# A late stage of attention without weight conversion, and a first token list made in two halves

## The chip, the cores and the metric

The kernel runs as one program on one core of a Trainium2 chip. The metric is the device time of one execution in microseconds (us). The engines are named as the profile names them: PE (TensorE), PEld (its weight loads), DVE (VectorE), ACT (ScalarE), POOL (GpSimd) and SP (SyncE, which here only issues DMAs). They run beside each other, each through its own list of instructions in a fixed order.

## The reference

```
x   = windowed attention(q, k, v)            # 4 x 8 heads, 576 rows, window 128, slope bias
logits = x @ w_gate                          # 2304 tokens x 8 experts
# greedy: (token, expert) pairs by falling logit; a token goes once, an expert takes at most 288
for e in experts: out[tokens of e] = relu(x[tokens] @ w1[e]) @ w2[e]
y = (silu(out @ w_gate2) * (out @ w_val)) @ w_out        # 512 -> 1536 -> 512
```

Each expert takes exactly 288 tokens, so the greedy choice can be made expert by expert: the expert that fills up first is found, its 288 tokens are listed, they are taken out, and so on, eight times.

## The kernel before, in words

**Two plans.** All work is described as tasks: engine, modelled duration, due time, what is read and written. `Plan.run` takes the tasks, always starts the one that can start first by its model, prefers early due times among those that can start about together, and so writes the order of every engine's list. There are two runs of it. The first covers attention (`plan.run(FIT[0], need)`): it ends when every attention task (`need`) is placed, and it fills gaps with the conversion of GLU weights (`glu_weights`, chunks 0 to `EARLY_GLU - 1`). The second covers everything else. The model holds no clock changes of PE and no lock between DVE and POOL other than its own "port".

**GLU weights.** 36 chunks of 512 KB go through three staging buffers (`stg`). On DVE each takes a shift (L329), a join (L332) and a sum (L344, or L348 for the last twelve chunks); for the first 24 DVE then forms the low half (L357). ACT does two conversions per chunk (L298). Chunks from `EARLY_GLU` on are loaded after the first gathers; chunks in `HOLD` get a tiny POOL memset into their buffer first (`hold`), which stands behind the gathers in POOL's list, so that SP can't start their load earlier.

**Attention.** 80 steps (4 batches x 5 row blocks x 4 head pairs). A step does scores on PE (L550), the maximum on DVE (L558), the exponential on ACT (L564), transposes on PE (L570), the split of the result in a high and a low float16 half, and products with the values on PE (L610). The split is done by ACT and DVE (L581, L585). In the steps of `VIA` (n mod 5 is 2 or 4) it goes by ACT (L590), POOL or DVE (L301) and POOL (L598). Every second step is followed by a normalization: ACT copies the sums (L654), DVE takes the reciprocal (L657), scales (L662) and sums the logits (L666). The normalized rows are stored to `x_dram` by SP.

**The first list, `route(0)`.** A chain on DVE, with a product on PE in each link: a search in six digits (compare L766, in two halves for the first list; count on PE L773; L841, PE L847, next digit), then positions (L882 to L928). Then `onehot` (L931) compares `k_slot`, a float16 table [128, 128, 18], with the positions, and `listed` (L936) makes the list with 18 small products, one for each of 18 tiles; `listed2` (L941 to L945) writes the indices. `k_slot` is filled once, by POOL (L301, called at L723). `CH` is cleared by POOL (L719). Gaps of the chain are filled with weight conversions. For the planner the chain can't start until all constants are there, `k_slot` among them; the instructions themselves wait for it only at `onehot`.

**The first expert.** `tokens(0)` issues three gathers on POOL (L1103: two of 128 rows of 2 KB, one of 128 quarter rows). Between the list and the gathers' landing stand `WARM` tasks: 12 products of no use (L1117), which keep PE busy. PE then turns the rows around (L1128, nine transposes in three pieces), ACT and DVE copy them (`X`), and the products of the expert follow (L1179: two layers in float32 for the first expert; L1174: GLU; L1309: output). For the seven later experts the lists, gathers and turns are made in the middle of the previous expert's products; the planner puts a turn where its model says that the gather has landed: `LATE` = 1.6 us after the transfer.

Of the kernel before, what the change touches and what calls it, by code (L numbers as in the profile page):

```python
# [9 lines left out]
F32 = mybir.dt.float32  # L10
F16 = mybir.dt.float16
# [38 lines left out]
FIT = (0.2, 0.1)  # L50

VIA = (5, (2, 4))
WARM = 6
EARLY_GLU = 11
HOLD = range(11, 14)

STEPS, FINE = (6, 6, 5, 5, 5, 5), (2, *10 * (3,))

# [66 lines left out]
class Plan:  # L125
# [15 lines left out]
    def add(self, engine, us, due, fn, r=(), w=(), late=0.0, soft=False, port=False):  # L141
        t = {"on": engine if isinstance(engine, dict) else {engine: us}, "due": due, "fn": fn, "late": late, "soft": soft, "port": port,
             "no": self.count, "deps": [], "next": [], "slots": [], "done": None}
        self.count += 1
        deps = {}
        for key in (*r, *w):
            if key in self.writer:
                deps[self.writer[key]["no"]] = self.writer[key]
        for key in w:
            for d in self.readers.get(key, ()):  # L150
                deps[d["no"]] = d
        for key in r:
# [12 lines left out]
        return t  # L165
# [24 lines left out]
                    s = max(s, max(u["done"] + u["late"] + HANDS.get(engine, 0.2) for u in users))  # L190
        return s

    def run(self, fit, need=None, near=0.0):

        todo = [t for t in self.todo if t["done"] is None]
        left = len(todo) if need is None else sum(t["done"] is None for t in need)
        ids = None if need is None else {t["no"] for t in need}
        ready = [t for t in todo if not t["wait"]]
        while left:
            by = {}  # L200
            busy = None if ids is None else {e for t in todo if t["done"] is None and t["no"] in ids for e in t["on"]}
            for t in ready:
                for e, us in t["on"].items():
                    if busy is not None and e not in busy:
                        continue
                    s = self.start(t, e)
                    if s is not None:
                        by.setdefault(e, []).append((t["due"], t["no"], s, us, t))
            best = None
            for e, c in by.items():  # L210
                s0 = min(x[2] for x in c)
                c = [x for x in c if not x[4]["soft"] or x[2] <= s0 + fit]
                first = min(c)
                fits = [x for x in c if x[2] + x[3] <= first[2] + fit or (e == "DVE" and x[2] + 0.1 < first[2] and x[0] < first[0] + near)]
                if fits:
                    s0 = min(x[2] for x in fits)
                    first = min(x for x in fits if x[2] <= s0 + fit)
                if best is None or first[2] < best[0][2]:
                    best = first, e
            (_, _, s, us, t), e = best  # L220
            t["ran"], t["done"] = e, s + us
            self.free[e] = s + us
            if self.ported(t, e):
                self.free["port"] = s + us
            for name in t["slots"]:
                if not self.slots[name]["taken"]:
                    self.slots[name]["taken"] = True
                    self.order[name[0]].append(name)
            ready.remove(t)
            for u in t["next"]:  # L230
                u["wait"] -= 1
                if not u["wait"]:
                    ready.append(u)
            left -= ids is None or t["no"] in ids
            t["fn"](e)
        self.todo = [t for t in todo if t["done"] is None]
        return max(self.free.values())
# [6 lines left out]
def dve(n, lanes=1):  # L244
    return 0.07 + n / 960 / lanes


def pool(n, ins=1):
    return 0.08 + n * ins / 940
# [11 lines left out]
def body(ctx, tc, a, out):  # L261
# [17 lines left out]
    k_tri = const.tile([128, 128], F16, name="k_tri")  # L279
    k_sum = const.tile([128, 3 * E], F16, name="k_sum")  # L280
    logits = const.tile([128, NT, E], F32, name="logits")
    x_dram = dram.tile([N, DM], F32, name="x_dram")

    def load(due, dst, src, nbytes, r=(), w=()):
# [11 lines left out]
    def copy_scaled(engine, dst, src, scale):  # L296
        if engine == "ACT":
            nc.scalar.activation(dst, src, AF.Copy, scale=scale)  # L298
        else:
            eng = nc.vector if engine == "DVE" else nc.gpsimd  # L300
            eng.tensor_scalar(dst, src, scale, 1.0, op0=OP.mult, op1=OP.mult)  # L301
# [75 lines left out]
    with ExitStack() as es:  # L377
# [13 lines left out]
        def due(n, off=0.0):  # L391
            return ATT_US * n + off
# [29 lines left out]
        for b in range(1, B):  # L422
# [7 lines left out]
        add("Pool", 0.2, due(40), lambda e: nc.gpsimd.tensor_copy(k_tri, cst[:, at["tri"]]), [("cst",)],  # L430
            [("cst", "tri")])

        add("Pool", 0.1, due(40), lambda e: nc.gpsimd.tensor_copy(k_sum, cst[:, at["sum"]]), [("cst",)],
            [("cst", "sum")])

# [101 lines left out]
        def step(n, b, kt, hp):  # L537
# [84 lines left out]
            for p in pars:  # L622
# [2 lines left out]
            cols = 128 * len(slots)  # L625
            add("PE", 0.109 * len(slots), due(n, 2.4), turn,
                r=[("ident",), ("PBz", n % NPB)] + [("PB", n, p) for p in pars], w=[("t", n)])
            if n % VIA[0] in VIA[1]:
                vi = vias[0]
                vias[0] += 1  # L630
                add("ACT", act(cols, True), due(n, 3.0), whole, r=[("t", n)], w=[("tf", vi)])
                add({"Pool": pool(cols), "DVE": dve(cols, 2)}, None, due(n, 3.2), high2, r=[("tf", vi)], w=[("th", n)], port=True)
                add("Pool", pool(cols, 2), due(n, 3.4), low2, r=[("tf", vi), ("th", n)], w=[("tl", n)])
            else:
                add("ACT", act(cols, True), due(n, 3.0), high, r=[("t", n)], w=[("th", n)])
                add("DVE", dve(cols), due(n, 3.6), low, r=[("t", n), ("th", n)], w=[("tl", n)])
# [56 lines left out]
        need = list(plan.todo)  # L693
        for c in range(EARLY_GLU):
            glu_weights(c, 2000 + c)
        plan.run(FIT[0], need)

# [12 lines left out]
    def rest_of(k):  # L710
# [3 lines left out]
    csum = const.tile([128, 1], F32, name="csum")  # L714
    bst = const.tile([128, NT], F32, name="bst")
    code = const.tile([128, NT], F32, name="code")
    CH = const.tile([128, NT // 3, 32], F16, name="CH")
    big = ctx.enter_context(tc.tile_pool(name="big", bufs=1))
    add("Pool", 0.7, U0 - 60, lambda e: nc.gpsimd.memset(CH, 0.0), w=[("CH",)])  # L719
    k_slot = big.tile([128, 128, NT], F16, name="k_slot")  # L720

    onehots = big.tile([128, 128, NT], F16, name="oc")
    add("Pool", pool(128 * NT), U0 - 40, lambda e: copy_scaled(  # L723
        e, k_slot, cst[:, at["slot"], None].to_broadcast([128, 128, NT]), 1.0), [("cst",)], [("cst", "slot")])
    rw = ctx.enter_context(tc.tile_pool(name="rw", bufs=2))
    wk = ctx.enter_context(tc.tile_pool(name="mwk", bufs=2))
# [6 lines left out]
    def route(k, due0, due1):  # L733
# [193 lines left out]
            for j in range(3):  # L927
                V.scalar_tensor_tensor(rh[:, :, j], v["pos"], 128.0 * j + 0.5, k_tok, op0=OP.is_gt, op1=OP.mult)  # L928

        def onehot():  # L930
            V.tensor_tensor(onehots, k_slot, v["po"][:, None, :].to_broadcast([128, 128, NT]), op=OP.is_equal)  # L931

        def listed():
            v["pi"] = rp.tile([128, 64], F32, name="rp")
            for t in range(NT):
                nc.tensor.matmul(v["pi"][:, :3], onehots[:, :, t], v["rh"][:, t, :], start=(t == 0),  # L936
                                 stop=(t == NT - 1))

# [78 lines left out]
        do("DVE", 0.7, place2)  # L1017
        do("DVE", 0.6, place3)
        do("DVE", 0.27, place4)
        do("DVE", dve(NT * 128, 2), onehot)  # L1020
        do("PE", 1.2, listed, w=[("listed",)] if k == 0 else [])
        do("DVE", 0.3, listed2, w=[("idx", k)])
        if k < E - 1:
            do("DVE", 0.3, close1)
# [68 lines left out]
    def tokens(k, u):  # L1093
# [14 lines left out]
        for c in range(3):  # L1108
            add("Pool", 1.03, u - ta, lambda e, c=c: fetch(e, c),
                r=[("idx", k)] + [("x_dram", b, kt) for b in range(B) for kt in range(5)], w=[("xg", k, c)], port=None)  # L1110
            add("DMA", 0.55, u - ta, lambda e: None, w=[("xg", k, c)], late=LATE)
        for i in range(WARM if k == 0 else 0):

            def warm(e):
                p = bank()
                for x in range(2):
                    nc.tensor.matmul(p, k_ones, GV[:, 0, 0, x], start=True, stop=True)  # L1117

            add("PE", 0.6, U0 - 30, warm, r=[("listed",)], w=[("mm", ("warm", i))])


        def turn(e, c, kd):
# [10 lines left out]
        for n, piece in enumerate(pieces):  # L1133
            add("PE", 0.11 * len(piece), u - ta + 4 + tn * n, lambda e, piece=piece: [turn(e, *x) for x in piece],
                r=[("xg", k, c) for c, _ in piece] + [("ident",)], w=[("mm", (k, "x", kd), c) for c, kd in piece], soft=k > 0)

        def ends(kd):

# [297 lines left out]
```

## Time and profile before

| | us |
|---|---|
| median of 3 runs (840.08 to 843.21) | 841.53 |
| the profiled execution, its own time | 841.45 |
| its span, first to last instruction | 839.7 |

PE is busy for 94% of the span, DVE for 73%, ACT for 41%, POOL for 17%. The chain of work that ended last spends 39% of the span in the products of L1174 alone. Attention ends near 139 us, the first list and its gathers take until 173 us, and from there to the end products follow one another. Start times are counted from the first instruction; a busy time of an engine over a stretch can be set against the stretch; the number in brackets behind a row of the timeline is the idle time of that engine before it and what ended it. [...]

### The profile page before, as it was taken

To read this page: it belongs to the slowest core of one execution; us is meant where nothing else is said; L and a number is where in the kernel's file an instruction comes from. 1 tells how busy PE (TensorE), PEld (TensorE's weight loads), DVE (VectorE), ACT (ScalarE), POOL (GpSimd) and SP (SyncE) were. 2 spreads that over 40 slices of the span, in tenths; PEclk is the share of its full clock that TensorE was granted. 3 is DMA by queue.
4 is the path that set the end of the run, shared out by engine and by line. 5 is a ranking of instruction groups with operands and counts; after the bars stand their busy time and mean duration, and the time that the engine had idled before them with its cause. 6 is when DMAs were issued, how large, how long until landed. Compare 5 with 4: busy or idle time off the path is not lost.

```text
span 839.7 us, 16655 instructions
## 1 busy us (share of the span) xinstructions
PE 791.2 (94%) x6373; PEld 583.5 (69%) x6373; DVE 614.5 (73%) x1795; ACT 345.2 (41%) x782; POOL 139.4 (17%) x200
## 2 busy tenths in 40 slices
PE   7999995489999999999999999999999999999997
PEld 6888884257774778577767865777677677757763
DVE  3788899979998988788878886889788864312320
ACT  5788884236445724412341243124312453312220
POOL 5677753100001000100110011001100120010001
PEclk9999998589999999999999999999999999999999
DMA  8889612468664002400330043004201561000001
GB/s 271 306 305 329 223 59 82 139 203 282 189 220 153 27 1 101 141 14 1 130 125 1 2 155 113 1 2 160 95 1 35 185 216 49 2 27 1 1 2 38
DMA packets 32064, 92.08 MB, mean 110 GB/s; under 512 B 3952, under 2 KB 10480, under 8 KB 31216
## 3 DMA queue, kind: packets, MB, share of 16 engines
q1 hardware_dynamic: 29008, 81.57, 29.1%
q0 software_dynamic: 2976, 9.44, 3.4%
q8 instruction: 50, 0.82, 0.4%
q14 instruction: 30, 0.25, 0.1%
HBM read 81.56 MB, written 9.44 MB: 108 GB/s over the span
## 4 chain that ended last, share of the span: by engine, by line
PE 55%; issue 10%; DVE 7%; DMA 4%; ACT 1%; POOL 1%; POOLq 0%; SPq 0%; DVEq 0%; ACTq 0%
PE mm L1174 39%; PE mm L1313 9%; PE mm L1179 4%; DMA xg<-x_dram,idx 2%; DMA stw<-in_w_dram 2%; DVE cn L808 1%; DVE cmp L804 1%; PE mm L1309 1%; PE mm L1128 1%; DVE P L1086 1%; PE rp L936 1%; DVE WE L1062 1%; ACT WE L1058 0%; PE rp L812 0%; POOL out_dram L1322 0%
## 5 line engine op out<-in xcount | busy, mean ns | idle before, releaser
L1174 PE MATMUL mm<-O,GV 128*128 128x288 f16 x2304 | 288.2, 286 | 0.5 <-DVE O L1088 0.5
L1174 PEld LDWEIGHTS <-GV 128*128 128x128 f16 x2304 | 221.9, 98 | 56.3 <-issue 0.9
L1174 PEld LDWEIGHTS <-WE 128*128 128x128 f16 x1344 | 130.0, 98 | 34.7 <-issue 1.4
L1313 PE MATMUL mm<-WO,P 128*128 128x512 f16 x504 | 112.9, 379 | 0.0
L1260 ACT ACTIVATE P<-z 128x288 f16<-128x288 f32 x84 | 37.1, 442 | 128.6 <-DVE z L1252 128.4
L1103 POOL DMA_INDIRECT xg<-x_dram,idx x24 | 25.3, 1053 | 386.0 <-PE mm L1174 172.4
L1062 DVE SCALAR_TENSOR_TENSOR WE<-stw,WE 128x512 f16<-128x512 f32 x112 | 74.5, 687 | 17.0 <-ACT WE L1058 17.0
L1313 PEld LDWEIGHTS <-P 128*128 128x128 f16 x504 | 48.9, 98 | 53.8
L1174 PE MATMUL mm<-P,WE 128*128 128x288 f16 x672 | 84.6, 286 | 0.0
L1174 PE MATMUL mm<-X,WE 128*128 128x288 f16 x672 | 83.9, 286 | 0.3 <-ACT X L1157 0.3
L1058 ACT ACTIVATE WE<-stw 128x1024 f16<-128x1024 f32 x56 | 58.5, 1055 | 30.6 <-DMA stw<-in_w_dram 30.5
L1252 DVE SCALAR_TENSOR_TENSOR z<-mm,t 128x288 f32<-128x288 f32 x84 | 38.0, 453 | 41.8 <-PE mm L1174 38.1
L808 DVE TENSOR_REDUCE cn<-cmp 128x56 f16<-128x1008 f16 (+2 forms) x55 | 63.6, 1157 | 0.5
L550 PE MATMUL s<-kt,qb 128*128 128x192 f32 (+2 forms) x288 | 57.4, 334 | 5.2 <-DMA kt<-in_kT_dram 4.2
L804 DVE TENSOR_TENSOR cmp<-wm,thr 128x1008 f16<-128x1008 f32 (+1 forms) x50 | 61.0, 1221 | 1.3
L1246 ACT ACTIVATE t<-mm 128x288 f32<-128x288 f32 x96 | 39.2, 409 | 51.6 <-PE mm L1174 49.4
L564 ACT ACTIVATE pb<-sc,mx 128x192 f32<-128x192 f32 (+2 forms) x144 | 56.2, 431 | 9.7 <-DVE mx L558 9.2
L1322 POOL DMA_INDIRECT out_dram<-R,idx x16 | 17.6, 1098 | 238.2 <-ACT R L1318 223.5
L1263 DVE TENSOR_TENSOR P<-z,P 128x288 f16<-128x288 f32 x84 | 38.2, 455 | 19.1 <-ACT P L1260 18.8
L558 DVE CUSTOM_DVE_ANT_0 sc<-s,bias 128x192 f32<-128x192 f32 (+2 forms) x144 | 41.8, 329 | 13.5 <-PE s L550 11.8
L550 PEld LDWEIGHTS s<-kt,qb 128*128 128x128 f32 x288 | 46.1, 201 | 7.6 <-DMA qb<-in_qB_dram 4.8
L1086 DVE SCALAR_TENSOR_TENSOR P<-mm,P 128x288 f16<-128x288 f32 x56 | 25.1, 453 | 31.0 <-ACT P L1081 30.7
(166 smaller groups left out, 1084.6 us busy)
## 6 DMA issues: line engine op xcount, KB each, us to landing
stw<-in_w_dram SPq DMA_DIRECT2D x56, 512.0 KB, 4.3
stg<-in_glu_dram SPq DMA_DIRECT2D x36, 512.0 KB, 4.0
qb<-in_qB_dram SPq DMA_DIRECT2D x3, 2304.0 KB, 9.9
x_dram<-xr SPq DMA_DIRECT2D x16, 256.0 KB, 3.4
WE<-in_w_dram SPq DMA_DIRECT2D x8, 512.0 KB, 4.9
kt<-in_kT_dram SPq DMA_DIRECT2D x3, 1152.0 KB, 6.1
vf<-in_vN_dram SPq DMA_DIRECT2D x8, 256.0 KB, 3.5
vt<-in_vT_dram SPq DMA_DIRECT2D x4, 512.0 KB, 7.4
```

What stands on the lines that cost most here:

```text
L550: nc.tensor.matmul(v["s"][:, par, c:], QB[b % 2][:, hp * 9 + i], KT[b % 2][:, hp, (i - 2) * 64 + c:(i + 1) * 64], start=True, stop=True)
L558: nc.vector.tensor_tensor_reduce(out=v["sc"][:, par, c:], in0=v["s"][:, par, c:], in1=bias[:, hp, c:], scale=-0.125, scalar=3.0e38, op0=OP ...
L564: nc.scalar.activation(PB[n % NPB][:, par, 64 * par + c:64 * par + W], v["sc"][:, par, c:], AF.Exp, bias=v["mx"][:, par:par + 1], scale=-1.0)
L804: V.tensor_tensor(v["ca"], v["wm"][:, :, None, :].to_broadcast(by), thr[:, None, :, None].to_broadcast(by), op=OP.is_ge)
L808: V.tensor_reduce(tile_of("cn", [128, E, 8], F16, bufs=1)[:, :, :n], v["ca"], op=OP.add, axis=AX.X)
L1058: nc.scalar.activation(WE[:, c, 0], v["f"], AF.Copy, scale=sc)
L1062: nc.vector.scalar_tensor_tensor(WE[:, c, 1, at], f[:, at], sc, WE[:, c, 0, at], op0=OP.mult, op1=OP.subtract)
L1174: nc.tensor.matmul(p[:, :CAP], w(i, k), x[:, j, k, :], start=(k == 0 and i == j), stop=(k == nk - 1 and j == 1))
L1246: nc.scalar.activation(v["t"], T["mm", k, ("gv", f, 0)][:, :CAP], AF.Silu, scale=1.0 / (SO * SG))
L1252: nc.vector.scalar_tensor_tensor(v["z"], T["mm", k, ("gv", f, 1)][:, :CAP], SPR / (SO * SG), v["t"], op0=OP.mult, op1=OP.mult)
L1263: nc.vector.tensor_sub(P()[:, 1, f], v["z"], P()[:, 0, f])
L1313: nc.tensor.matmul(T["mm", k, "y", c], x[:, i, kk, at], WO[0][:, kk, j, :], start=(kk == 0 and i == j), stop=(kk == 11 and i == 1))
```

## The change

- In the first plan's last `LAST` = 40 attention tasks no weight conversion and no weight load is placed (they stay for the second plan).
- The last three attention steps no longer go by POOL (of the three, steps 77 and 79 did).
- `k_slot` is filled by ACT, and `CH` is cleared by POOL earlier, in the middle of attention.
- `EARLY_GLU` is 10 instead of 11, and `HOLD` covers chunks 10 to 12 instead of 11 to 13: chunk 10 moves behind the first gathers.
- For the first list, `onehot` and `listed` come in two halves of nine tiles.
- Behind the first two of the three turns of the first expert's rows, six products of no use each.
- The planner counts gathers of all experts as landing 1.0 us later.

```
+LAST = 40
-EARLY_GLU = 11
-HOLD = range(11, 14)
+EARLY_GLU = 10
+HOLD = range(10, 13)
...
-    def run(self, fit, need=None, near=0.0):
+    def run(self, fit, need=None, near=0.0, last=0):
...
+            if ids is not None and left == last:
+                ready = [t for t in ready if t["no"] in ids]
...
-                if not u["wait"]:
+                if not u["wait"] and (ids is None or left > last + 1 or u["no"] in ids):
...
-            if n % VIA[0] in VIA[1]:
+            if n % VIA[0] in VIA[1] and n < 20 * B - 3:
...
-        plan.run(FIT[0], need)
+        plan.run(FIT[0], need, last=LAST)
...
-    add("Pool", 0.7, U0 - 60, lambda e: nc.gpsimd.memset(CH, 0.0), w=[("CH",)])
+        add("Pool", 0.7, due(40), lambda e: nc.gpsimd.memset(CH, 0.0), w=[("CH",)])
...
-    add("Pool", pool(128 * NT), U0 - 40, lambda e: copy_scaled(
+    add("ACT", act(128 * NT), U0 - 40, lambda e: copy_scaled(
         e, k_slot, cst[:, at["slot"], None].to_broadcast([128, 128, NT]), 1.0), [("cst",)], [("cst", "slot")])
...
-            V.tensor_tensor(onehots, k_slot, v["po"][:, None, :].to_broadcast([128, 128, NT]), op=OP.is_equal)
+            V.tensor_tensor(onehots[:, :, at], k_slot[:, :, at], v["po"][:, None, at].to_broadcast([128, 128, at.stop - at.start]),
+                            op=OP.is_equal)
...
+        if k == 0:
+            for at in (slice(0, 9), slice(9, NT)):
+                do("DVE", dve(9 * 128, 2), lambda at=at: onehot(at), w=[("oc", at.start)])
+            for at in (slice(0, 9), slice(9, NT)):
+                do("PE", 0.6, lambda at=at: listed(at), r=[("oc", at.start)], w=[("listed",)], chain=at.start > 0)
...
-            add("DMA", 0.55, u - ta, lambda e: None, w=[("xg", k, c)], late=LATE)
+            add("DMA", 0.55, u - ta, lambda e: None, w=[("xg", k, c)], late=LATE + 1.0)
+        def warm(e, n):
+            p = bank()
+            for x in range(n):
+                nc.tensor.matmul(p, k_ones, GV[:, 0, 0, x % 2], start=True, stop=True)
...
+            if k == 0 and n < 2:
+                add("PE", 0.21 * WARM, u - ta + 4 + tn * n + 0.1, lambda e: warm(e, WARM),
+                    r=[("mm", (k, "x", kd), c) for c, kd in piece], w=[("mm", ("warm", 10 + n))])
```

## Rows read from the trace of the kernel before

**Rows 1.** The profile page: span of the profiled execution.
```profile
span 839.7 us, 16655 instructions
...
```
**Rows 2.** Stretches: length; busy us (instructions) by engine; PE clock; DMA share; GB/s.
```profile
139.00:140.00 1.00, 0.00 (x0) 0.00 (x0) 0.90 (x4) 0.00 (x0) 0.00 (x0) 0.67 0.13 33
...
173.00:174.00 1.00, 0.63 (x2) 0.45 (x2) 1.00 (x3) 0.28 (x1) 0.10 (x1) 0.74 0.82 324
...
180.00:181.00 1.00, 1.00 (x5) 0.82 (x4) 1.00 (x4) 0.00 (x0) 0.00 (x0) 0.85 0.98 397
...
175.00:180.00 5.00, 5.00 (x14) 2.73 (x14) 2.51 (x8) 1.49 (x3) 0.13 (x2) 0.50 0.61 170
...
220.00:840.00 620.00, 605.51 (x4487) 431.22 (x4485) 433.38 (x1094) 205.52 (x407) 42.69 (x57) 1.00 0.22 71
```
**Rows 3.** Timeline of DVE, end of attention: start, us, instruction, tiles, shapes, idle before.
```profile
131.81 0.81 DVE L332 SCALAR_TENSOR_TENSOR cvt<-stg,cvt 128x512 int32<-128x512 int32 x1
...
134.90 0.69 DVE L344 CUSTOM_DVE_ANT_0 cvt<-cvt,cvr 128x1024 uint16<-128x1024 uint16 x1
135.51 2.35 DVE L329 TENSOR_SCALAR cvt<-stg 128x512 int32<-128x512 int32 x1
137.89 0.17 DVE L657 RECIPROCAL r<-r 64x4 f32<-64x4 f32 x1
...
138.94 0.06 DVE L958 MEMSET csum<- 128x1 f32 x1
```
**Rows 4.** Timelines of ACT, POOL and PE, the same end.
```profile
135.41 0.17 ACT L654 ACTIVATE r<-o 64x4 f32<-64x4 f32 x1 [1.48 <-PE o L610]
...
135.47 2.11 POOL L301 TENSOR_SCALAR k_slot<-cst 128x2304 f16<-128x2304 f32 x1 [0.48 <-PE o L610]
...
134.85 0.22 PE L610 MATMUL o<-vh,tl 128*64 128x73 f16 x1 [0.36 <-POOL tl L598]
```
**Rows 5.** Timelines of DVE and PE, a compare and the end of the first list.
```profile
140.69 1.40 DVE L766 TENSOR_TENSOR cmp<-bst,cst 128x567 f16<-128x567 f32 x2
...
160.75 1.35 DVE L931 TENSOR_TENSOR oc<-k_slot,po 128x2304 f16<-128x2304 f16 x1
162.02 0.68 DVE L332 SCALAR_TENSOR_TENSOR cvt<-stg,cvt 128x512 int32<-128x512 int32 x1
162.62 0.42 DVE L329 TENSOR_SCALAR cvt<-stg 128x512 int32<-128x512 int32 x1
...
163.56 0.14 DVE L941 TENSOR_SCALAR p<-rp 128x2 f32<-128x2 f32 x1
...
162.15 1.28 PE L936 MATMUL rp<-rh,oc 128*128 128x3 f16 x18 [4.12 <-DVE oc L931]
```
**Rows 6.** Timelines of POOL and PE, gathers, products of no use, turns, first products.
```profile
167.69 1.44 POOL L1103 DMA_INDIRECT xg<-x_dram,idx  x1 [0.30 <-DVE w L753]
...
163.30 4.39 PE L1117 MATMUL mm<-GV,k_ones 128*128 128x512 f16 x12
168.55 0.63 PE L1128 MATMUL mm<-cst,xg 128*128 128x128 f32 x4 [0.86 <-PE mm L1117]
171.10 0.66 PE L1128 MATMUL mm<-cst,xg 128*128 128x128 f32 x4 [1.93 <-DMA xg<-x_dram,idx]
...
172.89 0.30 PE L1128 MATMUL mm<-cst,xg 128*128 128x128 f32 x1 [0.86 <-DMA xg<-x_dram,idx]
173.56 2.29 PE L1179 MATMUL mm<-X,WE 128*128 128x288 f32 x4 [0.37 <-ACT X L1152]
```
**Rows 7.** Timelines of POOL and PE, the second expert's gather, turn and first product.
```profile
254.54 0.95 POOL L1103 DMA_INDIRECT xg<-x_dram,idx  x1 [71.15 <-DVE idx L944]
...
262.37 0.98 PE L1128 MATMUL mm<-cst,xg 128*128 128x128 f32 x7 [2.07 <-DMA xg<-x_dram,idx]
...
274.25 7.59 PE L1174 MATMUL mm<-X,WE 128*128 128x288 f16 x60 [0.34 <-ACT X L1157]
```
**Rows 8.** Waits of PE from 220 us on: us in total, times, longest.
```profile
PE mm L1128 <- DMA xg<-x_dram,idx: 3.3, 4, 2.1
```

More of the change, by code (lines that the diff above doesn't have):

```diff
@@ L281, in body @@
     logits = const.tile([128, NT, E], F32, name="logits")
+    CH = const.tile([128, NT // 3, 32], F16, name="CH")
     x_dram = dram.tile([N, DM], F32, name="x_dram")
@@ L716, in body @@
     code = const.tile([128, NT], F32, name="code")
-    CH = const.tile([128, NT // 3, 32], F16, name="CH")
     big = ctx.enter_context(tc.tile_pool(name="big", bufs=1))
-    add("Pool", 0.7, U0 - 60, lambda e: nc.gpsimd.memset(CH, 0.0), w=[("CH",)])
     k_slot = big.tile([128, 128, NT], F16, name="k_slot")
     onehots = big.tile([128, 128, NT], F16, name="oc")
-    add("Pool", pool(128 * NT), U0 - 40, lambda e: copy_scaled(
+    add("ACT", act(128 * NT), U0 - 40, lambda e: copy_scaled(
         e, k_slot, cst[:, at["slot"], None].to_broadcast([128, 128, NT]), 1.0), [("cst",)], [("cst", "slot")])
@@ L928, in place4, with onehot, listed @@
                 V.scalar_tensor_tensor(rh[:, :, j], v["pos"], 128.0 * j + 0.5, k_tok, op0=OP.is_gt, op1=OP.mult)
-        def onehot():
-            V.tensor_tensor(onehots, k_slot, v["po"][:, None, :].to_broadcast([128, 128, NT]), op=OP.is_equal)
-        def listed():
-            v["pi"] = rp.tile([128, 64], F32, name="rp")
-            for t in range(NT):
+        def onehot(at=slice(0, NT)):
+            V.tensor_tensor(onehots[:, :, at], k_slot[:, :, at], v["po"][:, None, at].to_broadcast([128, 128, at.stop - at.start]),
+                            op=OP.is_equal)
+        def listed(at=slice(0, NT)):
+            if at.start == 0:
+                v["pi"] = rp.tile([128, 64], F32, name="rp")
+            for t in range(at.start, at.stop):
                 nc.tensor.matmul(v["pi"][:, :3], onehots[:, :, t], v["rh"][:, t, :], start=(t == 0),
@@ L1019, in route @@
         do("DVE", 0.27, place4)
-        do("DVE", dve(NT * 128, 2), onehot)
-        do("PE", 1.2, listed, w=[("listed",)] if k == 0 else [])
+        if k == 0:
[3 more added lines that the diff above has]
+                do("PE", 0.6, lambda at=at: listed(at), r=[("oc", at.start)], w=[("listed",)], chain=at.start > 0)
+        else:
+            do("DVE", dve(NT * 128, 2), onehot)
+            do("PE", 1.2, listed)
         do("DVE", 0.3, listed2, w=[("idx", k)])
@@ L1110, in tokens @@
                 r=[("idx", k)] + [("x_dram", b, kt) for b in range(B) for kt in range(5)], w=[("xg", k, c)], port=None)
-            add("DMA", 0.55, u - ta, lambda e: None, w=[("xg", k, c)], late=LATE)
-        for i in range(WARM if k == 0 else 0):
[L1114 to L1119, printed above, removed]
+            add("DMA", 0.55, u - ta, lambda e: None, w=[("xg", k, c)], late=LATE + 1.0)
[3 more added lines that the diff above has]
+                nc.tensor.matmul(p, k_ones, GV[:, 0, 0, x % 2], start=True, stop=True)
+        for i in range(WARM if k == 0 else 0):
+            add("PE", 0.6, U0 - 30, lambda e: warm(e, 2), r=[("listed",)], w=[("mm", ("warm", i))])
         def turn(e, c, kd):
```

## The prediction

> **What bounds the kernel now.** I read the page first: the span is 839.7 us [rows 1] and the execution's own time 841.45, so 1.75 us lie around the span; the median of the runs is 841.53, and I take the two for equal. Then the table of stretches: from 220 us to the end PE is busy for 605.51 of 620 us at full clock [rows 2]. Nothing of the change touches that work, so there it can win only in the 14.5 us that PE idles, of which waits for gathers are 3.3 us in 4 waits [rows 8]. What is left is the stretch from the end of attention to the first products, where PE has little to do, DVE's chain sets the pace and the clock is low: the timelines by engine show which instruction is late at each step. Everything that starts the first expert's products sooner moves the rest with it, as long as PE finds no new wait later.
>
> **The change part by part**
>
> *A. End of attention.* ACT's last copy of sums starts at 135.41 and takes 0.17 [rows 4], so the reciprocal could start at 135.65. It starts at 137.89, because DVE has two conversion steps before it, and the second, a shift, takes 2.35 us, beside POOL's fill of `k_slot` from 135.47 to 137.58 [rows 3, 4]. The same shift takes 0.42 elsewhere [rows 5]. This is 137.89 - 135.65 = 2.24 us. `LAST` takes both steps and the join at 131.81 out, and `k_slot` leaves POOL. Before that, PE's last products wait 0.36 us for POOL [rows 4]. Without POOL's step and the join of 0.81 us [rows 3], DVE's low halves come as soon as ACT's high ones. That moves PE's end by 0.36 (the wait alone) to 1.17 us (with all of the join); I take 0.85, as the join partly lies beside PE's own work. The first instruction of the list chain, at 138.94 [rows 3], comes 2.24 + 0.85 = 3.1 us earlier. Bounds: -2.2 (only the lock goes) to -3.5.
>
> *B. What the planner puts in front of the list.* The chain waits for `k_slot` in the model. On POOL, `k_slot` held the model's port, and no conversion could be placed beside it; on ACT (2.0 us in the model) it leaves DVE some 1.2 us of modelled time in which conversions fit: a join and a shift. Their real price is start to start 162.62 - 162.02 = 0.60 and 0.42 less overlap, 0.34 [rows 5]: +0.9. Bounds: 0 (nothing is ready) to +2.0 (a third step). ACT itself is idle there (0.00 us in 139 to 140 [rows 2]), and `onehot` reads the table some 22 us later, so its 2 us are hidden. The three steps moved out of attention cost 0.60 + 0.60 + 0.34 = 1.5 us of DVE's time in all; two of them are B, the rest falls in gaps of the chain or later (F).
>
> *C. The list in halves.* Now the compare takes 1.35 and PE's 18 products 1.28 after it; the indices start at 163.56 behind conversions [rows 5]. In halves PE starts after about 0.67 us, and its second half ends 1.28 / 2 = 0.64 after the second compare instead of 1.28 (a second instruction costs DVE about 0.07): -0.55, of which DVE's fillers leave -0.5. If the halves, rows of nine elements at a pitch of 18, ran at the rate of the compares on float32 (2 x 567 elements in 1.40 us [rows 5], so 1152 in 1.3 to 1.4), the second would end 1.3 us later than now and the list +0.6. Bounds -0.6 and +0.6; I take the row of the same instruction, -0.5.
> [...]
>
> *D. Gathers and turns.* The three turns start at 168.55, 171.10 and 172.89; the last two wait for their gathers, 1.93 and 0.86 us [rows 6]. Chunk 10's 512 KB no longer run beside the second gather, though beside the third; its load on SP, and the loads of expert weights behind it, now wait for a POOL memset that stands behind three gathers, as chunk 11's did. The chunk's first use, in the GLU products, lies far behind that. I take -0.3, bounds 0 to -1.0. The six products behind each of two turns stand in PE's list ahead of the next turn. [...] I take +0.2. The conversions pushed back may also stand beside POOL's gathers, of which one took 1.44 us where the later one at 254.54 took 0.95 [rows 6, 7]; up to +0.5, taken as nothing.
>
> *E. PE's clock.* It falls in the microsecond from 173 on (mean 0.74), after a stretch with gaps of 1.93 and 0.86 us between turns, and comes back in the one from 180 on (0.85) [rows 2, 6]. So it is low from about 173.5 to 180.3. [...] It had also fallen in the microsecond from 139 on (0.67), when PE had stood still since attention's last products [rows 2, 4]. With products between the turns there is hardly a gap left from 163 on, and I expect it to stay up: -3.2. Bounds 0 and -3.3.
>
> Up to here: -3.1 + 0.9 - 0.5 - 0.1 - 3.2 = -6.0 us.
>
> *F. The second expert's gather.* PE waits 2.07 us for it [rows 7]. PE comes there 6.0 us earlier; does the gather? Its list hangs on DVE, which is nearly full. DVE starts 3.1 earlier with 1.5 us more to do, and of 5 us from 175 to 180 it is busy for only 2.51 [rows 2], since its chain waits there for slow PE, which E cures. So the second list comes 4 to 5 us earlier, the wait would grow by 1 to 2 us, and the planner, which now counts the landing 1.0 us later, puts more output products in front: I take +0.9. Bounds -2.0 (no wait is left) and +2.6 (the list gains only 1.6).
>
> *G. Later gathers.* 3.3 - 2.07 = 1.2 us of waits [rows 8] which turns placed later can avoid: -0.6, bounds -1.2 and +1.0 (another order puts something else late; new orders of experts 2 to 8 come without a row).
>
> Sum: -6.0 + 0.9 - 0.6 = -5.7 from 841.45: 835.8; I say 836.0.
>
> **The rivals**
>
> *R1, the clock falls all the same.* For it: it came back only after 6.7 us of products [rows 2, 6], and a few products between turns may not be enough; a third gap of 0.37 before the first product stays [rows 6]. Against it: the products fill just the gaps after which it fell. E is then 0, DVE's chain is as slow as now (F +0.2 instead of +0.9), and D costs 0.5 more: 836.0 + 3.2 - 0.7 + 0.5 = 839.0.
>
> *R2, DVE hands it back.* The moved steps are not saved, only moved, and the second list gains no more than 3.1 - 1.5 = 1.6 us. PE, 6.0 us early, waits 4.4 us longer at the turns, less the 1.8 us of products now placed before: F is +2.6, and the time 836.0 + 1.7 = 837.7. Against it: the idle half of DVE from 175 to 180.
>
> *R3, the other side.* The later landing holds for all experts. From some point, where the model sees the turns behind the last output product, an expert's first product waits for its whole gather and copy. The second expert stands near it: its last turn comes just before its first product, which waits 0.34 us for the copy [rows 7]. If seven experts waited as the second does for its gather, 2.07 us [rows 7], that were 14.5 us against a gain of some 5: 851. It decides from three to four experts on. Against it: the wait is 3.3 us in all now, and output products are left to be put in front.
>
> *R4, it doesn't do what it says.* The planner refills in front of the list what `LAST` took out (B at 2.0), and the halves are ordered so, or run so, that the list is no shorter (C at +0.6): 836.0 + 1.1 + 1.1 = 838.2.
>
> **How the numbers follow.** Forecast 0.55 (its own range 833 to 838), R1 0.20, R2 0.12, R4 0.08, R3 0.05. About 0.5%, 4.2 us, is what a measurement of this kernel can tell from no change; the line is at 837.3. Below it lie 0.85 of the forecast's chance, a third of R2's and R4's and a tenth of R1's: 0.47 + 0.07 + 0.02, with a little for gains that I don't see, 0.58. Slower is R3 and a little: 0.06. Same: 0.36. The range: above 840.5 lie R3 and a part of R1, 0.11; below 832.0, where F and G are at their good ends, 0.08.
>
> **What would show it.** A: the first instruction of the chain near 136.7 (135.8 and two conversions), the shift there 0.4 us. C: two compares of about 0.7 us, products between them. D, E: granted clock 1.0 from about 166 to the end, first product near 170.6, its four at 1.1 us. F: the second expert's turns wait 2 to 4 us. The forecast is wrong if the clock is low after the first product, if the halves take over a microsecond each, or if PE's idle time from 220 us on grows by more than 2 us.

## The result and the profile after

| | before | after |
|---|---|---|
| median of four runs each (us) | 841.89 (840.08 to 843.21) | 833.66 (832.81 to 833.71) |
| the profiled execution, its own time | 841.45 | 833.71 |
| its span | 839.7 | 831.9 |

The ratio is 0.9901, 95% interval [0.9881, 0.9921]: 8.2 us faster, where 5.7 were forecast. The total is inside the range, but the terms of the sum erred against each other, and the experiments are mostly about that.

The page of the changed kernel, its span:

```profile
span 831.9 us, 16685 instructions
```

The table of stretches of the changed kernel, columns as in [rows 2]. PE's granted clock, as a share of full speed, is 1.00 where it was 0.74, 0.50 and 0.85, and DVE is busy for 4.80 of the 5 us from 175 on (2.51 before). From 220 us to the end PE idles for 611.90 - 601.29 = 10.6 us; before it was 14.5, of which 0.3 lay behind the end of the span.

```profile
173.00:174.00 1.00, 0.77 (x3) 0.67 (x4) 1.00 (x4) 0.18 (x1) 0.31 (x6) 1.00 1.00 393
175.00:180.00 5.00, 5.00 (x22) 3.71 (x21) 4.80 (x12) 2.21 (x5) 0.00 (x0) 1.00 0.89 295
180.00:181.00 1.00, 1.00 (x6) 0.79 (x5) 1.00 (x3) 0.95 (x3) 0.00 (x0) 1.00 0.28 78
220.00:831.90 611.90, 601.29 (x4457) 428.87 (x4454) 430.02 (x1085) 202.84 (x403) 46.00 (x57) 1.00 0.21 70
```

The timeline of DVE in the changed kernel, end of attention, beside [rows 3]: the shift of 2.35 us is gone and the last reciprocal waits for ACT alone, but a join and two shifts (L336, L333) stand between the last logits (L671) and the chain's first instruction (L963).

```profile
134.62 0.17 DVE L662 RECIPROCAL r<-r 64x4 f32<-64x4 f32 x1
...
135.46 0.42 DVE L590 SCALAR_TENSOR_TENSOR tl<-t,th 128x256 f16<-128x256 f32 x1
136.71 0.17 DVE L662 RECIPROCAL r<-r 64x4 f32<-64x4 f32 x1 [0.82 <-ACT r L659]
...
137.44 0.26 DVE L671 TENSOR_REDUCE logits<-lgp 64x8 f32<-64x64 f32 x1
137.73 0.69 DVE L336 SCALAR_TENSOR_TENSOR cvt<-stg,cvt 128x512 int32<-128x512 int32 x1
138.34 0.76 DVE L333 TENSOR_SCALAR cvt<-stg 128x512 int32<-128x512 int32 x2
...
139.04 0.06 DVE L963 MEMSET csum<- 128x1 f32 x1
```

PE and ACT at the same end, beside [rows 4]: PE's last products now wait 0.62 us for DVE, and ACT fills `k_slot` where it has nothing else to do.

```profile
135.94 0.22 PE L615 MATMUL o<-vh,tl 128*64 128x73 f16 x1 [0.62 <-DVE tl L590]
...
136.50 0.17 ACT L659 ACTIVATE r<-o 64x4 f32<-64x4 f32 x1 [1.49 <-PE o L615]
136.70 2.12 ACT L302 ACTIVATE k_slot<-cst 128x2304 f16<-128x2304 f32 x1
```

DVE and PE at the end of the first list, then PE up to the first products, beside [rows 5, 6]. The two halves start at 160.93, and the instruction behind them at 162.73. The second turn waits for nothing, and the first expert's first four products take 1.24 us in place of 2.29.

```profile
160.93 1.96 DVE L934 TENSOR_TENSOR oc<-k_slot,po 128x1152 f16<-128x1152 f16 x2
162.73 0.69 DVE L336 SCALAR_TENSOR_TENSOR cvt<-stg,cvt 128x512 int32<-128x512 int32 x1
...
163.70 0.16 DVE L946 TENSOR_SCALAR p<-rp 128x2 f32<-128x2 f32 x1
...
162.01 0.72 PE L941 MATMUL rp<-rh,oc 128*128 128x3 f16 x9 [3.79 <-DVE oc L934]
162.94 0.72 PE L941 MATMUL rp<-rh,oc 128*128 128x3 f16 x9 [0.21 <-DVE oc L934]
163.52 4.50 PE L1127 MATMUL mm<-GV,k_ones 128*128 128x512 f16 x12
168.67 0.63 PE L1139 MATMUL mm<-cst,xg 128*128 128x128 f32 x4 [0.66 <-PE mm L1127]
169.14 1.46 PE L1127 MATMUL mm<-GV,k_ones 128*128 128x512 f16 x6
170.43 0.60 PE L1139 MATMUL mm<-cst,xg 128*128 128x128 f32 x4
...
173.23 1.24 PE L1193 MATMUL mm<-X,WE 128*128 128x288 f32 x4 [0.37 <-ACT X L1166]
```

POOL and PE at the second expert's gather, beside [rows 7]: the gather starts only 1.8 us earlier, and yet its turns wait for nothing.

```profile
252.75 0.95 POOL L1114 DMA_INDIRECT xg<-x_dram,idx  x1 [78.77 <-PE mm L1323]
...
260.14 1.04 PE L1139 MATMUL mm<-cst,xg 128*128 128x128 f32 x8
...
268.63 3.27 PE L1188 MATMUL mm<-X,WE 128*128 128x288 f16 x24 [0.36 <-ACT X L1171]
```

PE's waits from 220 us on, beside [rows 8]; these two lines are all that the view lists. No gather is among them.

```profile
PE rp L815 <- DVE cn L811: 3.6, 8, 1.2
PE mm L1188 <- ACT X L1171: 0.4, 1, 0.4
```

### The profile page after: what moved, and what is told of

The parts are those of the page before. It is cut to its first block, busy times and chain, and to the rows that moved or that the text cites. A ratio compares the mean times of both kernels' runs of the same rounds, so it can differ in the third digit from the quotient of the medians.

```text
span 831.9 us, 16685 instructions
## 1 busy us (share of the span) xinstructions
PE 790.0 (95%) x6385; PEld 583.5 (70%) x6385; DVE 615.0 (74%) x1797; ACT 347.0 (42%) x783; POOL 138.1 (17%) x196
## 4 chain that ended last, share of the span: by engine, by line
PE 61%; DVE 17%; issue 11%; DMA 4%; ACT 3%; POOL 1%; SPq 1%; POOLq 0%; DVEq 0%; ACTq 0%
PE mm L1188 39%; PE mm L1327 9%; PE mm L1193 2%; PE s L555 2%; DVE cmp L807 2%; DVE cn L811 2%; PE mm L1323 2%; PE o L615 2%; DVE WE L1073 1%; DMA stw<-in_w_dram 1%; PE t L575 1%; DMA qb<-in_qB_dram 1%; DVE sc L563 1%; DVE tl L590 1%; DMA x_dram<-xr 1%
## 5 line engine op out<-in xcount | busy, mean ns | idle before, releaser
L1336 POOL DMA_INDIRECT out_dram<-R,idx x16 | 20.5, 1284 | 228.6 <-ACT R L1332 215.0
```

## The experiments

All were timed in five rounds beside the kernel before. Attention ends earlier or later from one execution to the next even where its instructions are the same: in the profiles of the changed kernel, e1, e2, e6, e7 and e8 the last logits start between 135.83 (e2) and 139.03 us (e8). So steps are measured from their own start: from the last logits to the chain, from the chain to the index `p`, from `p` to the first product.

| | median (range, runs), us | ratio to before |
|---|---|---|
| e1 | 830.66 (830.19 to 833.41, 6) | 0.9867 [0.9845, 0.9890] |
| e2 | 837.00 (834.26 to 839.20, 6) | 0.9925 [0.9901, 0.9949] |
| e3 | 833.44 (833.01 to 834.16, 6) | 0.9895 [0.9875, 0.9915] |
| e4 | 839.95 (837.84 to 843.01, 12) | 0.9974 [0.9958, 0.9990] |
| e5 | 836.68 (835.12 to 838.62, 6) | 0.9947 [0.9927, 0.9967] |
| e6 | 831.05 (830.48 to 833.59, 6) | 0.9894 [0.9872, 0.9916] |
| e7 | 830.64 (829.51 to 831.74, 5) | 0.9884 [0.9862, 0.9905] |
| e8 | 835.65 (832.91 to 838.03, 6) | 0.9935 [0.9911, 0.9959] |
| e9 | 839.92 (837.50 to 842.25, 12) | 0.9976 [0.9956, 0.9996] |
| e10 | 837.56 (834.79 to 840.65, 12) | 0.9960 [0.9942, 0.9979] |
| e11 | 833.37 (831.80 to 835.06, 6) | 0.9894 [0.9874, 0.9914] |
| e12 | 830.74 (828.79 to 832.20, 6) | 0.9868 [0.9846, 0.9889] |

**e1: the changed kernel without the products behind the turns.**

```
-            if k == 0 and n < 2:
-                add("PE", 0.21 * WARM, u - ta + 4 + tn * n + 0.1, lambda e: warm(e, WARM),
-                    r=[("mm", (k, "x", kd), c) for c, kd in piece], w=[("mm", ("warm", 10 + n))])
```

> The changed kernel without the six products behind each of the first two turns; all else as changed. Theory 1 (these products keep the clock up, and that is over a third of the gain): the clock falls again near 173.5 us and is low for 6 to 7 us, the first product starts at about 173, the products of the first expert end 3 us later than in the changed kernel; time 833.7 + 3.1 = 836.8. Rival (the gaps are shorter because chunk 10 no longer loads beside the gathers, so the clock stays up without them): 833.7 within 0.7, first product up to 0.3 us earlier.

Measured: 830.66, faster than the changed kernel by 3. PE's timeline in this kernel shows gaps between the turns of 0.83 and 0.29 us in place of 1.93 and 0.86, and the clock does not fall (1.00 from 173 to 174 us). So in the changed kernel the twelve products are not what keeps the clock up. They cost: from `p` to the first product it is 8.37 us here (162.85 to 171.22) and 9.53 there (163.70 to 173.23), 1.2 of the 3.

```profile
167.87 0.63 PE L1139 MATMUL mm<-cst,xg 128*128 128x128 f32 x4 [0.17 <-PE mm L1127]
169.33 0.66 PE L1139 MATMUL mm<-cst,xg 128*128 128x128 f32 x4 [0.83 <-DMA xg<-x_dram,idx]
...
170.55 0.30 PE L1139 MATMUL mm<-cst,xg 128*128 128x128 f32 x1 [0.29 <-DMA xg<-x_dram,idx]
171.22 1.24 PE L1190 MATMUL mm<-X,WE 128*128 128x288 f32 x4 [0.37 <-ACT X L1163]
```

A stretch of e1, columns as in [rows 2]:

```profile
173.00:174.00 1.00, 1.00 (x6) 0.55 (x5) 0.79 (x4) 0.78 (x2) 0.14 (x4) 1.00 1.01 410
```

**e2: the changed kernel with the landing as before.**

```
-            add("DMA", 0.55, u - ta, lambda e: None, w=[("xg", k, c)], late=LATE + 1.0)
+            add("DMA", 0.55, u - ta, lambda e: None, w=[("xg", k, c)], late=LATE)
```

> The changed kernel with gathers planned to land as early as before (1.6 instead of 2.6 us after the transfer). Theory 1 (planning the turns later takes away PE's waits for gathers): PE waits 2 us or more for the second expert's gather and about 1.2 us for later ones again; 833.7 + 3.3 = 837.0. Rival (those waits went because PE and VectorE keep another pace when the clock stays up, or because loads moved): the waits stay under 1 us in all, 833.7 within 0.8.

Measured: 837.0, 3.3 us more than the changed kernel. PE's waits from 190 us on have the gathers again, and more of them than [rows 8]. The profiled execution took 839.20, the longest of the six, so 5.4 us is a high value:

```profile
PE mm L1139 <- DMA xg<-x_dram,idx: 5.4, 8, 2.0
```

**e3: the kernel before with the products behind the turns and the later landing**, the last two hunks of the change and nothing else.

> The kernel before with two edits alone: six products behind each of two turns, and the later planned landing. Theory 1 (the edits in attention's end, the list in halves and chunk 10 earn nothing): 841.9 - 8 = 833.9, as fast as the changed kernel within 0.7. Rival (the prediction's terms A to C, 2.7 us, are in the gain): 841.9 - 5.5 = 836.4 or slower. A third outcome, faster than the changed kernel by 0.2 to 0.5 us, would say that the other edits cost something: the halves, 0.15 us by the trace.

Measured: 833.44, as fast as the changed kernel. The clock stays up (1.00 from 173 to 181 us), and waits for gathers are 0.5 us in all from 190 us on. With these two in place, all the rest of the change can be left out without loss.

**e4: the kernel before with only the end of attention changed** (`LAST`, the last steps off POOL, `k_slot` on ACT).

```
+LAST = 40
...
-            if n % VIA[0] in VIA[1]:
+            if n % VIA[0] in VIA[1] and n < 20 * B - 3:
...
-    add("Pool", pool(128 * NT), U0 - 40, lambda e: copy_scaled(
+    add("ACT", act(128 * NT), U0 - 40, lambda e: copy_scaled(
```

> The kernel before with the edits in attention's end alone: no conversion in its last 40 tasks, no step by GpSimd in the last three, the table filled by ScalarE. Theory 1 (three conversions stand in front of the list's chain instead): chain starts at 139.0 within 0.4 us, time 841.9 within 0.7. Rival (terms A and B as predicted, -2.2): chain starts near 136.8, time 839.7.

Measured: 839.95, -0.26% [-0.42, -0.10], some 2 us in the median. The end of attention is shortened as in the changed kernel, and three conversions stand ahead of the chain there too. The two steps together earn 0.7 us (2.0 - 1.3); the interval reaches from 0.8 to 3.5 us, and where the rest comes from is not shown. In the profiled execution, one of the longer of the twelve (842.40), the turns wait 2.07 and 2.60 us for their gathers, and the clock falls; the stretch of [rows 2] in this kernel:

```profile
175.00:180.00 5.00, 5.00 (x13) 2.88 (x14) 1.65 (x5) 0.44 (x2) 0.13 (x2) 0.50 0.32 104
```

**e5: e1 with chunk 10 loaded as before.**

```
-EARLY_GLU = 10
-HOLD = range(10, 13)
+EARLY_GLU = 11
+HOLD = range(11, 14)
```

> As e1 (the changed kernel without products between turns), and chunk 10 loads as before, ahead of the first gathers (chunks 11 to 13 held instead of 10 to 12). Theory 2 (chunk 10's load beside the gathers made the gaps between the turns, and the gaps let the clock fall; moving it is what keeps the clock up in e1): from the list's end to the first product 11 to 12.7 us instead of 8.4, clock low for 6 to 7 us after that, time 830.7 + 3 to 5 = 834 to 836. Rival (the clock stayed up in e1 by its moment, not by the load): 830.7 within 1.

Measured: 836.68, a little above the 834 to 836 of theory 2 and 6 us more than e1 (the intervals of the two ratios lie apart: 0.9927 to 0.9967, 0.9845 to 0.9890), and as much more than e6 and e7, which have chunk 10 behind the gathers and were timed beside e5. PE's timeline and SP's queue in this kernel: two loads of 512 KB are issued in the stretch of the gathers (the row begins at 163.97 and spans 4.22 us), and the second and third turn wait 2.02 and 3.47 us. From the third gather's start on POOL to its turn it is 7.86 us here (168.31 to 176.17), 3.56 in e1 (166.99 to 170.55).

```profile
169.13 0.63 PE L1139 MATMUL mm<-cst,xg 128*128 128x128 f32 x4 [0.94 <-PE mm L1127]
171.77 0.66 PE L1139 MATMUL mm<-cst,xg 128*128 128x128 f32 x4 [2.02 <-DMA xg<-x_dram,idx]
...
176.17 0.45 PE L1139 MATMUL mm<-cst,xg 128*128 128x128 f32 x1 [3.47 <-DMA xg<-x_dram,idx]
...
163.97 4.22 SPq L329 DMA_DIRECT2D stg<-in_glu_dram  x2
```

The stretch behind them in e5 has the clock at 0.50:

```profile
174.00:180.00 6.00, 3.47 (x9) 2.09 (x10) 1.24 (x4) 0.80 (x2) 0.23 (x1) 0.50 0.46 147
```

SP's queue in e1, for comparison: one load before the gathers, the next two behind them.

```profile
162.65 0.34 SPq L329 DMA_DIRECT2D stg<-in_glu_dram  x1
...
169.55 3.33 SPq L329 DMA_DIRECT2D stg<-in_glu_dram  x2
```

Between e1 and e5, neither of which has the products, it is thus chunk 10's place that decides on the clock (1.00 and 0.50). With the products the clock is 1.00 from 173 to 181 us even where chunk 10 is loaded as before (e3, e9). Chunk 10's place alone is not always enough: e8 shows a case.

**e6: e1 with the list in one piece.**

```
-            for at in (slice(0, 9), slice(9, NT)):
-                do("DVE", dve(9 * 128, 2), lambda at=at: onehot(at), w=[("oc", at.start)])
...
+        do("DVE", dve(NT * 128, 2), onehot)
+        do("PE", 1.2, listed, w=[("listed",)] if k == 0 else [])
```

> As e1, with the first list's compare and its 18 products in one piece each, as before. Theory 2 (the halves run at 0.90 us each, not 0.67, and give back what the overlap wins): list as long as in e1 within 0.2 us, time 830.7 within 0.7. Rival (the halves win the predicted 0.5 us, hidden in the traces by conversions): list 0.5 us longer, 831.2 or more.

Measured: 831.05 against e1's 830.66: no difference. From the chain's start to `p` it is 24.67 us here (137.82 to 162.49) and 24.65 in e1 (138.20 to 162.85): the halves shorten nothing. PE's last product of the list ends no earlier either, 2.69 us after the compare's start here (159.68; 161.09 + 1.28) and 2.74 in e1 (160.07; 162.09 + 0.72). With the halves DVE gets one conversion less done before `p`, two instead of three.

**e7: e1 with the table laid out so that each half is one run.**

```
-    k_slot = big.tile([128, 128, NT], F16, name="k_slot")
+    k_slot = big.tile([128, 2, 128, NT // 2], F16, name="k_slot")
...
-    onehots = big.tile([128, 128, NT], F16, name="oc")
+    onehots = big.tile([128, 2, 128, NT // 2], F16, name="oc")
```

> As e1, with the table and the compare's result laid out so that each half of nine tiles is one run of 1152 elements (now rows of 9 at a pitch of 18). Theory 2 (the pitch of 18 costs the halves their rate): each half 0.67 us, the list's indices 0.5 us earlier than in e1, time 830.7 - 0.5 = 830.2. Rival (rows of nine in the second operand, or the half's odd length, cost it): halves stay at 0.9 us, 830.7 within 0.7.

Measured: 830.64. On DVE's timeline the next instruction starts 1.47 us after the halves' start, not 1.80, and from the chain's start to `p` it is 24.27 us (138.32 to 162.59), 0.38 less than in e1. In the time of the kernel that can't be told from e1.

```profile
160.19 1.55 DVE L936 TENSOR_TENSOR oc<-k_slot,po 128x1152 f16<-128x1152 f16 x2
161.66 0.69 DVE L336 SCALAR_TENSOR_TENSOR cvt<-stg,cvt 128x512 int32<-128x512 int32 x1
```

**e8: e7, and in the plan only the compare waits for `k_slot`, not the chain.**

```
-    consts = [("cst",), ("cst", "tab"), ("cst", "ones"), ("cst", "unit"), ("cst", "tri"), ("cst", "sum"), ("cst", "slot")]
+    consts = [("cst",), ("cst", "tab"), ("cst", "ones"), ("cst", "unit"), ("cst", "tri"), ("cst", "sum")]
...
-                do("DVE", dve(9 * 128, 2), lambda at=at: onehot(at), w=[("oc", at.start)])
+                do("DVE", dve(9 * 128, 2), lambda at=at: onehot(at), r=[("cst", "slot")], w=[("oc", at.start)])
```

> As e7, and the plan no longer holds the first list's chain back until the table is filled (only the compare that reads it waits). Theory 2 (three conversions, 1.28 us, stand in front of the chain only because the plan makes it wait for the table): the chain starts 0.3 us after attention's last logits instead of 1.6, time 1.3 us below e7, near 829. Rival (the conversions are needed early enough that they come back in the chain's gaps or later): chain starts early, its length grows by as much, time as e7 within 0.5.

Measured: 835.65, a miss: 5 us slower than e7. The three conversions do go from in front of the chain, which starts 0.32 us after the last logits (139.03 to 139.35). But all that follows is planned anew. The tenth load of GLU weights from the start, chunk 9, is issued at 167.29 us, beside the gathers, after SP has waited 7.0 us for a join of DVE (L336), which reads a staging buffer; in e7 the tenth is issued at 162.42 and the next one at 169.28, behind the gathers. And the clock falls to 0.53, as the stretch of this kernel shows. The second and third turn wait only 0.50 and 0.64 us for gathers, but between the first and the second PE also waits 1.14 us for a compare, and from the first turn to the first product it takes 4.58 us (168.51 to 173.09) where e7 takes 2.73 (167.77 to 170.50). That this load makes the clock fall fits with chunk 10's place in e5, but was not tested alone. The load, PE's wait for the compare, and the stretch:

```profile
167.29 0.34 SPq L329 DMA_DIRECT2D stg<-in_glu_dram  x1
...
170.28 0.34 PE L784 MATMUL rp<-cmp,CH 128*32 128x189 f16 x6 [1.14 <-DVE cmp L769]
...
173.00:174.00 1.00, 0.92 (x2) 0.77 (x3) 0.89 (x3) 0.79 (x3) 0.00 (x0) 0.53 1.04 381
```

**e9 and e10: the two hunks of e3, each alone.** e9 has the first of these, e10 the second:

```
+            if k == 0 and n < 2:
+                add("PE", 0.21 * WARM, u - ta + 4 + tn * n + 0.1, lambda e: warm(e, WARM),
...
-            add("DMA", 0.55, u - ta, lambda e: None, w=[("xg", k, c)], late=LATE)
+            add("DMA", 0.55, u - ta, lambda e: None, w=[("xg", k, c)], late=LATE + 1.0)
```

> The kernel before with one edit: six products of no use behind each of the first two turns. The landing that the planner counts stays as before. Both edits together (e3) earned 8.7 us. Theory 1: the two gains add. The landing earned 3.3 (e2 against the changed kernel), so the products alone earn some 5: 836 to 838, clock 1.0 from the first product on. Theory 2: they need each other. With the clock up PE comes to the second expert's gather over 3 us earlier, and without a later landing in the plan it waits that much longer there: the products alone earn 0 to 2, 840 to 842, and PE's waits for gathers rise from 3.3 to over 5 us.

> The kernel before with one edit: the planner counts each gather as landing 1.0 us later. Theory 1 (gains add): the clock falls in the first expert as before (0.50 in 175 to 180), PE's waits for gathers, 3.3 us before, fall under 1, and the time is 838.5 to 839.5. Theory 2 (they need each other): with the clock low the later landing takes away at most the 3.3 us of waits, so 839 as well; what tells the theories apart is that the two runs' gains add up to 8.7 by theory 1 and to some 4 to 5 by theory 2.

Measured: e9 839.92, -0.24% (2.0 us); e10 837.56, -0.40% (3.4 us); together 0.64% with an interval of about +-0.27 (the two intervals added in squares), where both at once (e3) give 1.05 +-0.20. The difference, 0.41 +-0.34%, is 3.4 us with an uncertain size; e9 and e10 share their runs of the kernel before (median 840.62), so even that interval is rather too narrow. By the medians alone they earn 0.7 and 3.1 us. In e9 the clock is 1.00 from 173 us on, and PE pays part of it back at the gathers: its waits are 4.5 us in 6 in place of 3.3 in 4. PE's waits in e9 from 190 us on:

```profile
PE mm L1128 <- DMA xg<-x_dram,idx: 4.5, 6, 2.1
```

The second expert's turn in e9 comes 2.4 us earlier than in [rows 7] and waits as long:

```profile
260.01 0.98 PE L1128 MATMUL mm<-cst,xg 128*128 128x128 f32 x7 [2.08 <-DMA xg<-x_dram,idx]
```

In e10 no wait for a gather is left behind 190 us, but the first expert's turns wait 1.40 and 2.57 us and the clock is 0.50. The last of these turns:

```profile
174.70 0.45 PE L1128 MATMUL mm<-cst,xg 128*128 128x128 f32 x1 [2.57 <-DMA xg<-x_dram,idx]
```

The stretch behind it in e10:

```profile
175.00:180.00 5.00, 4.63 (x12) 2.58 (x11) 1.36 (x3) 1.35 (x3) 0.13 (x2) 0.50 0.07 30
```

So theory 2 is the nearer one, that the two need each other: the sum is 5.4 us by the ratios and 3.8 by the medians, on either side of the 4 to 5 that it gave.

**e11 and e12: the changed kernel and e1, side by side.**

> The changed kernel itself, beside e12 on the same chip, to tell how much the products behind the turns cost. Theory 1: they stand on the path of the first expert and cost 2 to 3 us there: 833 to 834, e12 830.5 to 831.5. Theory 2: the 3 us between e1 and the changed kernel, which were timed in two comparisons, are the difference of two chips: e11 and e12 within 1 us of each other.

> The same kernel as e1: the changed kernel without the products behind the turns. Theory 1: 2 to 3 us less than e11, 830.5 to 831.5, with no overlap of most runs. Theory 2: within 1 us of e11.

Measured: 833.37 and 830.74, 2.6 us apart with little overlap. So the products behind the turns cost what e1 had shown, on another chip too. In the profiles of the changed kernel and e1, 1.2 us of it lie between `p` and the first product (9.53 and 8.37). Where the rest comes from, behind the first product, no run shows.

## Why the prediction was right in the total and wrong in its terms

| step | forecast, us | measured in the two profiles, us |
|---|---|---|
| A, end of attention | -3.1 | -2.0 |
| B, conversions ahead of the list | +0.9 | +1.3 |
| C, list in halves | -0.5 | 0.0 |
| D, gathers and turns | -0.1 | -0.5 |
| E, clock | -3.2 | -3.1 |
| F and G, gathers of experts 2 to 8 | +0.3 | some -3.6 |

**A: the mechanism held, the size did not.** The 2.24 us of the first part are gone: the shift took 2.35 us beside POOL's fill of `k_slot`, 0.42 at the median of its seven from 100 to 170 us in the kernel before, and the two beside ACT's fill (138.34) take 0.42 each. The second part, 0.85, is not there; what is measured is -2.0, from the third logits sum from the end (L666 at 127.69 before, L671 at 128.52 after) to the last (138.62 and 137.44: 10.93 and 8.92). With POOL's step and the join out of the way, DVE puts the normalization of the step before (134.62 to 135.4) ahead of the low half that PE waits for (135.46): PE's wait went from 0.36 for POOL to 0.62 for DVE.

**B: right in kind, one shift too few.** A join and two shifts came, 1.3 us from 137.73 to 139.04. e8 shows that they go if the plan does not hold the chain for `k_slot`.

**C: this step failed.** It took the pace of the whole table's compare (1.35 us for 2304 elements in [rows 5]) for the halves, 0.67 us each, and 0.07 for a second instruction, near what float32 compares of the kernel before show (1.40 for two of 567 in [rows 5], 1.34 for one of 1134 at 180.46). The halves take 1.80 / 2 = 0.90. That is nearer to 0.67 than to the upper bound (1.3), which is the pace of the float32 compares, and it is enough to undo the gain: from the chain's start to `p` it is 24.62 us before (138.94 to 163.56) and 24.66 after. e7 has the same elements in one run each, 1.47 / 2 = 0.74, and the list is 0.38 shorter, which is the term as forecast, nearly. So the rows of nine at a pitch of 18, in the table, in the result or in both, are what costs; the positions they are compared with come in rows of nine in e7 too. Why they cost it, no run shows. The second half is no slower than the first: PE's second nine products start 0.93 us after its first (162.01, 162.94), so the second compare took no longer than about 0.9.

**D: the total is right, the parts are not.** Moving chunk 10 was taken at -0.3 (bounds 0 to -1.0). It is far more: `p` to the first product takes 8.37 us in e1, with chunk 10 moved and no products, 12.80 in e5, with chunk 10 as before and no products (164.18 to 176.98), and 10.00 in the kernel before (163.56 to 173.56), which loads it early too and has no products, as e4 (12.67). No run shows the +0.2 that was taken for the products; six take 1.29 us (169.14 to 170.43) with the clock at 1.00, and together they cost some 1.2 (9.53 in the changed kernel, 8.37 in e1). The sum -0.5 hid both.

**E: the size is right, the cause given is only one of two.** The clock stays up (1.00 from 173 to 181 us). The term was the author's estimate of what 6.7 us at the lower clock cost, and no run shows it by itself; what the profiles show is four products in 2.29 us at a clock of 0.50 (176.03 before) and in 1.24 at 1.00 (174.58 after). Behind the first 64 products of the expert a count product stands at 193.08 before and at 189.64 after, 3.44 us earlier, where the first product is 0.33 earlier (173.56, 173.23); the difference is 3.1. The two rows, before and after:

```profile
193.08 0.34 PE L781 MATMUL rp<-cmp,CH 128*32 128x189 f16 x6
...
189.64 0.34 PE L784 MATMUL rp<-cmp,CH 128*32 128x189 f16 x6
```

The prediction said that products in the gaps do it. e9 shows that they can (clock 1.00 with chunk 10 as before), e1 that they need not where no load stands beside the gathers, e5 that with neither the clock falls. Of eight profiles without the products, the clock falls to 0.50 in five. In three of these SP's queue has a load of 512 KB of GLU weights issued between the start of POOL's first gather and the end of its third (the kernel before, e5, e8); the other two load chunk 10 as the kernel before does (e4, e10). It is 1.00 from 173 to 181 us in the three whose queue has none there (e1, e6, e7). The mean clock of all executions agrees, not only that of the profiled ones: 0.979 to 0.983 in e1 and in e9, 0.972 to 0.978 in e10, which has no products and chunk 10 as before. R1 is refuted, and no run shows the 0.5 that it adds to D.

**F: wrong sign, and the largest error.** The prediction said that the second list comes 4 to 5 us earlier and the wait grows. The gather starts 1.8 us earlier, nearly what R2 says (1.6), though not all for R2's reason: the list's last compare on DVE comes 2.7 us earlier (249.55, 246.89), but its products on PE only 1.6 (251.99, 250.39), because they stand in PE's list behind twelve output products instead of eight. And the wait did not grow: it is gone. What was mis-sized is the plan's answer. From the first output product to the second expert's turn, PE had 260.30 - 248.56 = 11.7 us before its wait began (262.37 - 2.07 in [rows 7]; the output product, L1309, starts at 248.56), and has 260.14 - 245.24 = 14.9 now: 32 output products stand in front instead of 24. The later landing does this alone too: e10 has 32, and e2, all of the change but the landing, has 28, with 5.4 us of waits for gathers and 3.3 us more time. **G** has the same cause: no later gather is waited for, and PE idles 10.6 us from 220 on, not 14.2 (to the end of the span).

The sum of the measured terms is -7.9. That the forecast of -5.7 came so near is luck in part: A, B and C came out 2.0 us worse than forecast, F and G 3.9 better. In the profiled pair attention came 0.8 us later in the run after, which leaves -7.1, and the span is 7.8 shorter: 0.7 us I can't place.

**The rivals.** R4 was right about what it named: A to C earned 0.7 us (2.0 - 1.3 - 0.0), not 2.7, and e4, with A and B alone, earned some 2 us (0.8 to 3.5) with the clock falling. It lost because F and G went the other way. R3 did not come: no expert waits for its gather.

**What beats both kernels.** e1, the changed kernel without the products behind the turns: 830.66 and 830.74 us, 11.4 and 11.1 below the kernel before in the same comparisons and 2.6 below the changed kernel beside it (e11, e12). e6 and e7 can't be told from it, so the halves may go too. A small change of the plan can lose this again: e8 differs from e7 only in what the chain waits for in the plan, and loses 5 us.

## What to carry to other kernels

Where a gap lets PE's clock fall, see first whether the gap can be shortened: in e1 one load of 512 KB moved from beside the gathers kept the clock up (1.00; 0.50 in e5) as twelve filler products do, without their 2.6 us. Then look where the other loads come to stand: in e8 another one came beside the gathers, and the clock fell to 0.53. A gain on PE's path was paid out in part at the next gathers that PE waits for (4.5 us in e9, 3.3 before): products alone earned some 2 us and the later landing alone some 3, both together 8.7. When a forecast hits its total, measure the terms; here errors of +2 and -4 us hid behind it, and the best kernel with them.

## What the runs showed that was not expected

- Two compares of 1152 float16 elements in rows of nine, at a pitch of 18, took 0.90 us each from start to start; as one run 0.74; the whole table of 2304 in one instruction 1.27 (160.75 to 162.02 in [rows 5]).
- In one link of the second list's search, whose chain alternates between DVE and PE, DVE's pace goes with the clock. DVE waits 2.01 and 0.98 us for small products on PE in the kernel before, at a clock of 0.50; the second of them (L847) stands in PE's list behind four products of the expert, which take 2.29 us:

```profile
176.14 0.16 DVE L841 TENSOR_SCALAR fu<-rp 63x8 bf16<-63x8 f32 x1 [2.01 <-PE rp L790]
...
178.47 0.17 DVE L852 TENSOR_REDUCE mx<-rp 128x1 f32<-128x8 f32 x1 [0.98 <-PE rp L847]
```

In the changed kernel, at a clock of 1.00, the four take 1.24 us, and the same two steps, with other conversions between them, wait for nothing:

```profile
175.06 0.15 DVE L844 TENSOR_SCALAR fu<-rp 63x8 bf16<-63x8 f32 x1
...
175.97 0.17 DVE L855 TENSOR_REDUCE mx<-rp 128x1 f32<-128x8 f32 x1
```
